# Leftover keys on GpSimd, attention output over two PSUM banks, and a later place for weight loads in a fused pooled-attention and MLP kernel

## The chip, the cores and the metric

One core of one Trainium2 chip. The metric is the device time of one execution in microseconds (us). Spans of the profile are about 1.7 us shorter than device times. TensorE, VectorE, ScalarE and GpSimd stand as PE, DVE, ACT and POOL in the profile; the queues that issue DMAs are SPq (SyncE), ACTq and POOLq.

## The reference, cut to what matters

```python
def _attn_ref(q, k, v):                         # (8, 8, 576, 64): batch, heads, sequence, head dim
    k_p = k.reshape(B, H, 72, 8, D).mean(axis=3)  # keys and values pooled by 8
    v_p = v.reshape(B, H, 72, 8, D).mean(axis=3)
    scores = scale * np.matmul(q, k_p.transpose(0, 1, 3, 2))
    ...                                           # softmax
    return np.matmul(attn, v_p)

def _moe_ref(x, w_in, w_out):                   # x: 4608 tokens of 512, w_in 512x2048
    h = x @ w_in
    g = h - np.tanh(h)
    return g @ w_out
```

So every batch needs its q, k and v loaded, k and v pooled, 72 pooled keys per head scored, and the result, 576 tokens, sent through two dense layers. The kernel handles the tokens in nine groups of 512.

## The kernel before

A group is 16 steps of h (four 128x512 matmuls each, then a tanh and a subtraction) and 16 steps of the output (four matmuls each). The attention of the next batch is woven between these matmuls. That works for groups 1 to 8. At the start there is nothing to weave it into: batch 0's attention must be done before group 0, and the weights arrive while group 0 runs. w1 (the first layer's weights) comes in four chunks of 512 KB, each for four steps of h; w2 likewise. GpSimd issues them; they are cast to bf16 on the way.

The first loads, with their queues:

```python
    load_main(k_pairs, k_raw[0], 0, 0, 1)               # SyncE: batch 0's keys, in three parts
    load_q0(0, 2)                                       # ScalarE: q by heads
    ...
    load_q0(4, 8)
    load_dense(k_pairs, k_raw[0], 0, nc.scalar)         # leftover keys: the last 16 of 144 rows of each head pair
    load_dense(v_pairs, v_raw[1], 0, nc.scalar)         # leftover values
    ...
    nc.gpsimd.memset(q_bf[64:128, R, :, :], 0.0)
    ...                                                 # masks
    nc.gpsimd.dma_start(out=v_bf[:, 0:NM, :], in_=v_pairs[0, 0:128, :, :])   # batch 0's v
    ...
    for c in range(4):
        load_w1(c)
    load_w2(0)
    nc.gpsimd.tensor_copy(out=v_bf[:, NM, :], in_=v_raw[1][:, NM, :])
    load_w2(1)
    ...
    after(load_k(1), w1_dmas[1])        # SyncE: batch 1's k behind w1's second chunk
    load_q(1, False)
    load_main(v_pairs, v_raw[1], 1, 0, NM)
```

Keys are pooled by three adds (4+4, 2+2, 1+1), tile by tile on VectorE; the leftovers are the fifth tile. The output of attention (AV) is then made in eight half blocks, each normalized on VectorE. Between them some steps of h are opened: the first two of their four matmuls run early, and the other two, the second halves of h, follow when AV is done. (kT are the pooled keys transposed, VB the pooled values as AV reads them; the q tail is the last 64 of a head's 576 rows of q.)

```python
    pool_k(0, nc.vector, 2, 4)
    warm_pe(6)                          # matmuls on zeros that fill a wait
    k_turn(2, 4)                        # transposes on TensorE, copies on VectorE
    pool_k(0, nc.vector, NM, NT)        # the leftover keys
    ...
    av_half(0, 0, 0, xs[0], ps_all)     # 3 matmuls, a reciprocal, a multiply
    ...                                 # eight of these, transposes and opened h between them
    for i in range(5, NHID):
        mlp_h(0, i, gts)
        if i == 7:
            q_pe_tail(0)                # the last 64 tokens of batch 0, inside h
        ...
        if i == 13:
            x_pe_transpose(0, 4, x4)
```

The softmax here doesn't subtract the row's maximum and nothing guards it: scores larger than these inputs give would overflow.

## Time and profile before

| | before |
|---|---|
| time, median of the first 3 runs | 300.77 us (300.72 to 301.53) |
| span in the profile | 299.1 us |
| AV's first matmul | 14.61 us |
| second halves of h begin | 21.27 us |
| group 1 begins | 54.98 us |
| w1's last chunk lands | 26.5 us |
| batch 1's v lands | 40.8 us |

The prediction below shows the lines that the starts of AV and of the second halves come from. In each row the first number behind the stretch is its length, then come busy us and, in brackets, instructions of PE, PEld, DVE, ACT and POOL, then the granted clock, the DMA share and GB/s.

```profile
core 0: us, PE busy (x) PEld busy (x) DVE busy (x) ACT busy (x) POOL busy (x), PEclk, DMA share, GB/s
0.00:14.60 14.60, 12.60 (x71) 5.56 (x71) 8.93 (x27) 8.64 (x15) 10.67 (x27) 1.00 0.99 239
14.60:21.30 6.70, 5.72 (x54) 3.59 (x55) 4.59 (x17) 2.85 (x9) 0.00 (x0) 1.00 1.23 212
21.30:55.00 33.70, 32.87 (x233) 17.13 (x232) 22.67 (x51) 21.68 (x39) 13.44 (x8) 1.00 1.11 281
55.00:240.00 185.00, 185.00 (x1046) 90.43 (x1045) 100.52 (x217) 91.92 (x180) 91.34 (x75) 1.00 0.72 177
```

Read it from the bottom. From 55 us on TensorE is busy for 185.00 of 185 us at full clock, so nothing that ends before can do more than move this block. Group 0 (third row) has 0.83 us without a matmul, the two waits of 0.32 and 0.52 us that the prediction names. The first two rows, 21.3 us, are what a change to the start can shorten, and there the DMA engines' mean busy share is 0.99 and more. (Packets are counted at their start, so a share can exceed 1.)

### The profile page before, as it was taken

The page shows a single profiled execution, that of the slowest core. Times are in us where ns is not written, and L with a number is a line of the kernel's source. Part 1 is how long each engine was busy: PE and PEld are TensorE (multiplying, and loading weights), DVE is VectorE, ACT ScalarE, POOL GpSimd, SP SyncE. Part 2 cuts the span into 40 slices and gives each one's busy share as a digit, 9 for nine tenths or more (in the row PEclk, how much of TensorE's full clock was granted, in tenths as well). Part 3 has the DMA queues.
Part 4 walks back from the last instruction along what each step waited for, and adds up shares of the span by engine and source line. Part 5 has one row for each costly group of instructions (what it writes and reads, how often), then busy time and mean ns, then how long its engine had stood idle before and what let it go on. Part 6 is the DMA issues. An engine that isn't in the chain of part 4 may idle for free.

```text
span 299.1 us, 4694 instructions
## 1 busy us (share of the span) xinstructions
PE 291.5 (97%) x1671; PEld 142.5 (48%) x1671; DVE 159.1 (53%) x343; ACT 149.4 (50%) x283; POOL 115.5 (39%) x110
## 2 busy tenths in 40 slices
PE   7989999999999999999999999999999999999994
PEld 3454455544544454445444554455445544444443
DVE  5658665673547444753476247716680758108600
ACT  4647583666146633654265516650665166126511
POOL 8500904871496109922971089307940000000000
PEclk9999999999999999999999999999999999999999
DMA  7999999849854998699648974897431430111032
GB/s 251 226 211 278 311 227 310 263 87 328 234 113 99 271 297 134 117 302 245 107 88 235 300 167 94 242 294 159 97 66 35 95 92 0 37 70 36 0 72 70
DMA packets 66183, 49.79 MB, mean 166 GB/s; under 512 B 39920, under 2 KB 52976, under 8 KB 66160
## 3 DMA queue, kind: packets, MB, share of 16 engines
q1 hardware_dynamic: 58832, 42.94, 56.0%
q0 software_dynamic: 4752, 4.72, 9.4%
q10 hardware_dynamic: 2576, 1.84, 2.3%
q8 instruction: 13, 0.21, 0.3%
q14 instruction: 10, 0.08, 0.1%
HBM read 36.70 MB, written 9.44 MB: 154 GB/s over the span
## 4 chain that ended last, share of the span: by engine, by line
PE 85%; DMA 9%; POOL 4%; issue 0%; SPq 0%; ACT 0%; DVE 0%; POOLq 0%
PE o_ps L456 40%; PE hT_ps L428 37%; DMA w1b<-in_moe_w_in_dram 4%; PE x_ps L346 4%; DMA k_raw<-in_k_dram 4%; PE s_ps L298 3%; POOL k_raw L198 1%; DMA out_dram<-o_sb 1%; POOL k_raw L203 1%; POOL kd L206 1%; POOL w2b L510 0%; PE xT_ps L390 0%; POOL v_raw L576 0%; PE qT_ps L171 0%; POOL w1b L503 0%
## 5 line engine op out<-in xcount | busy, mean ns | idle before, releaser
L456 PE MATMUL o_ps<-w2b,gT 128*128 128x512 bf16 x560 | 134.4, 380 | 0.0
L441 DVE TENSOR_TENSOR gT<-hT_ps,t_sb 128x512 bf16<-128x512 f32 x144 | 98.9, 691 | 57.7 <-ACT t_sb L439 57.6
L428 PE MATMUL hT_ps<-xT,w1b 128*128 128x512 bf16 x576 | 126.9, 379 | 0.3 <-ACT xT L397 0.3
L439 ACT ACTIVATE t_sb<-hT_ps 128x512 f32<-128x512 f32 x144 | 85.6, 597 | 38.3 <-PE hT_ps L428 37.5
L428 PEld LDWEIGHTS <-w1b 128*128 128x128 bf16 x576 | 55.9, 98 | 66.5 <-issue 0.4
L456 PEld LDWEIGHTS <-gT 128*128 128x128 bf16 x560 | 52.5, 98 | 52.0 <-issue 1.4
L465 ACT COPY o_sb<-o_ps 128x512 f32<-128x512 f32 x33 | 19.3, 585 | 75.2 <-PE o_ps L456 75.2
L359 DVE RECIPROCAL rden<-x_ps 128x4 f32<-128x4 f32 x80 | 14.2, 177 | 52.5 <-PE x_ps L346 52.0
L360 DVE TENSOR_TENSOR x_sb<-x_ps,rden 128x256 bf16<-128x256 f32 x80 | 34.0, 425 | 3.5 <-DMA xT<-x_sb 0.6
L148 POOL CAST q_bf<-q_raw 128x2048 bf16<-128x2048 f32 x6 | 11.3, 1888 | 59.9 <-issue 34.8
L198 POOL TENSOR_TENSOR k_raw<-k_raw 128x1280 f32<-128x1280 f32 x7 | 20.2, 2886 | 27.4 <-DMA k_raw<-in_k_dram 16.6
L317 ACT ACTIVATE E<-s_ps 128x288 bf16<-128x288 f32 x60 | 21.4, 410 | 13.2 <-PE s_ps L298 13.0
L346 PE MATMUL x_ps<-VB,E 128*128 128x130 bf16 x240 | 20.8, 221 | 0.4 <-ACT xT L397 0.3
L346 PEld LDWEIGHTS <-E 128*128 128x128 bf16 x240 | 16.9, 98 | 8.8 <-DVE VB L230 0.6
L216 POOL TENSOR_TENSOR v_raw<-v_raw 128x1280 f32<-128x1280 f32 x6 | 17.4, 2898 | 0.0
L298 PE MATMUL s_ps<-qT,KB 128*128 128x288 bf16 (+5 forms) x128 | 17.0, 290 | 0.2
L298 PEld LDWEIGHTS <-KB 128*128 128x128 bf16 (+1 forms) x128 | 7.0, 96 | 10.2 <-issue 3.5
L527 PE MATMUL warm_ps<-xT 128*128 128x512 bf16 x29 | 10.2, 465 | 1.3 <-DVE xT L539 1.3
L206 POOL TENSOR_TENSOR kd<-k_raw 128x640 bf16<-128x640 f32 x7 | 10.8, 1540 | 0.5
L203 POOL TENSOR_TENSOR k_raw<-k_raw 128x640 f32<-128x640 f32 x7 | 10.8, 1541 | 0.5
L397 ACT CAST xT<-xT_ps 128x256 bf16<-128x256 f32 (+1 forms) x14 | 5.8, 436 | 8.5 <-PE xT_ps L390 5.1
L219 POOL TENSOR_TENSOR v_raw<-v_raw 128x640 f32<-128x640 f32 x6 | 9.3, 1544 | 0.5
(73 smaller groups left out, 100.7 us busy)
## 6 DMA issues: line engine op xcount, KB each, us to landing
k_raw<-in_k_dram SPq DMA_DIRECT2D x7, 1024.0 KB, 5.9
q_raw<-in_q_dram SPq DMA_DIRECT2D x7, 1024.0 KB, 10.2
v_raw<-in_v_dram SPq DMA_DIRECT2D x7, 1024.0 KB, 9.3
out_dram<-o_sb SPq DMA_DIRECT2D x38, 128.0 KB, 2.4
out_dram<-o_sb SPq DMA_DIRECT2D x16, 256.0 KB, 3.7
w1b<-in_moe_w_in_dram POOLq DMA_DIRECT2D x4, 512.0 KB, 14.2
w2b<-in_moe_w_out_dram POOLq DMA_DIRECT2D x4, 512.0 KB, 16.9
k_raw<-in_k_dram SPq DMA_DIRECT2D x7, 128.0 KB, 5.8
```

The source lines that it names most:

```text
L198: first = eng.tensor_tensor(out=r[:, :, 0:4, :], in0=r[:, :, 0:4, :], in1=r[:, :, 4:8, :], op=ALU.add)
L216: eng.tensor_tensor(out=r[:, :, 0:4, :], in0=r[:, :, 0:4, :], in1=r[:, :, 4:8, :], op=ALU.add)
L298: nc.tensor.matmul(dst[p : p + w], lhsT=KB[b % 2][:, o : o + w], rhs=qTs[b][:, m, c0:c1], start=True, stop=True,)
L317: nc.scalar.activation(out=E[:, t, half * hs : (half + 1) * hs], in_=ps[:, :], func=ACT.Exp, scale=SCALE)
L346: nc.tensor.matmul(ps[:, 2 * n : 2 * n + 2, :].rearrange("p h d -> p (h d)") if n < 2 else ps.rearrange("p (a s) d -> p a s d", s=2)[:, :, ...
L359: nc.vector.reciprocal(out=rden[:, :, :], in_=ps[:, :, D:D1])
L360: nc.vector.tensor_tensor(out=x_sb[:, half, :, :], in0=ps[:, :, 0:D], in1=rden[:, :, :].to_broadcast([128, 4, D]), op=ALU.mult,)
L428: nc.tensor.matmul(h_tiles[i][:, :], lhsT=w1b[:, fb, i * 128 : (i + 1) * 128], rhs=xT[:, fb, tok0 : tok0 + TG], start=(fb == 0), stop=(fb ...
L439: nc.scalar.activation(out=t_sb[:, :], in_=h_ps[:, :], func=ACT.Tanh)
L441: nc.vector.tensor_sub(out=gT[:, :], in0=h_ps[:, :], in1=t_sb[:, :])
L456: nc.tensor.matmul(o_ps[:, :], lhsT=gts[i][:, tb * 128 : (tb + 1) * 128], rhs=w2b[:, i, :], start=(i == 0), stop=(i == NHID - 1),)
L465: (nc.vector.tensor_copy if g == 0 and tb % 2 else nc.scalar.copy)(out=o_sb[:, :], in_=o_ps[:, :])
```

## The change

Its intent is to shorten the start and to take the waits out of group 0. Five things move at once:

```diff
 # 1. GpSimd: w1 in three chunks, leftover keys pooled, the memset moved behind the load of v
-    nc.gpsimd.memset(q_bf[64:128, R, :, :], 0.0)
     nc.gpsimd.memset(mask[:, :, :], 1.0)
     ...
     nc.gpsimd.dma_start(out=v_bf[:, 0:NM, :], in_=v_pairs[0, 0:128, :, :])
+    nc.gpsimd.memset(q_bf[64:128, R, :, :], 0.0)
     ...
-    for c in range(4):
+    for c in range(3):
         load_w1(c)
-    load_w2(0)
+    pool_k(0, nc.gpsimd, NM, NT)
     nc.gpsimd.tensor_copy(out=v_bf[:, NM, :], in_=v_raw[1][:, NM, :])
-    load_w2(1)
 # 2. w1's last chunk and w2 behind batch 1's k and q; batch 1's v behind w2's first chunk
-    after(load_k(1), w1_dmas[1])
-    load_q(1, False)
-    load_main(v_pairs, v_raw[1], 1, 0, NM)
+    k1 = load_k(1)
+    after(k1[:1], w1_dmas[1])
+    load_dense(v_pairs, v_raw[1], 1)
+    load_q_tail(0)                       # was issued by ScalarE at 8 us
+    load_q_nine(1, 0, nc.sync)
+    load_q_nine(1, 1, nc.sync)
+    load_w1(3)
+    after(w1_dmas[3:], w1_dmas[2])
+    load_w2(0)
+    load_w2(1)
+    after([load_main(v_pairs, v_raw[1], 1, 0, NM)], w2_dmas[0])
+    pool_k(1, nc.gpsimd, 0, NM)
+    load_w2(2)
+    pool_k(1, nc.gpsimd, NM, NT)
+    load_w2(3)
 # 3. AV in four pairs of blocks, each over two PSUM banks
+    def av_pair(p, half, b0):
+        ps = PS[:, b0 : b0 + 2, 0 : 4 * D1].rearrange("p k (h d) -> p k h d", d=D1)
+        for k in range(2):
+            av_mms(0, 2 * p + k, half, ps[:, k, :, :])
+        ...                              # one reciprocal, one multiply for both
 # 4. batch 0's last 64 tokens: AV and transposes in the output's first steps
+        if i == 11:
+            q_cast_tail(0, nc.scalar.copy)
+        if i == 12:
+            q_four_tail(0)
     ...
         if u == 0:
+            x4 = av(0, 4, ps_any, False)
+        if u == 1:
+            x_pe_transpose(0, 4, x4)
 # 5. batch 1's q loaded as nine rows per partition, with no separate tail of 256-byte packets
+    q_nine = q.rearrange("b (s a h) (p j) d -> b s p a h (j d)", s=2, a=2, j=NJ)
 # cut: PSUM as one tile with a helper that hands out its banks; fewer filler matmuls; the five loads
 # that ScalarE issued between 13 and 17 us (batch 1's leftover values, q tail) are gone from its queue
```

## The prediction

> **What bounds the kernel now.** I read the page's busy shares and 40 slices first, then the chain that ended last in order of time, then the timelines of TensorE, VectorE, ScalarE and GpSimd over the first 56 us, then each load's time to landing.
>
> ```profile
> PE 291.5 (97%) x1671; PEld 142.5 (48%) x1671; DVE 159.1 (53%) x343; ACT 149.4 (50%) x283; POOL 115.5 (39%) x110
> ...
> PE   7989999999999999999999999999999999999994
> ...
> DMA  7999999849854998699648974897431430111032
> ```
>
> TensorE is full from the fourth slice on. From 55 us to the end a group is 64 + 64 matmuls of 128x512 plus the next batch's attention, with no wait; a change to the start can only move that block as a whole. The DMA row is also full for the first 50 us, so the loads' order matters. The chain shows where the start still hangs on data:
>
> ```profile
> 5.86 12.86 DMA w1b<-in_moe_w_in_dram
> 18.73 0.38 SPq L102
> 19.21 10.84 DMA k_raw<-in_k_dram
> ...
> 30.21 2.90 POOL k_raw L198
> 33.11 1.47 POOL w2b L510 x2
> 34.58 1.58 POOL k_raw L203
> 36.23 1.55 POOL kd L206
> 37.82 0.45 PE kT_ps L259 x5
> ```
>
> k of batch 1 lands at 30.05, GpSimd pools it until 37.78, and TensorE's transposes wait for that. After them the chain is TensorE alone. In TensorE's timeline the places that matter are:
>
> ```profile
> 11.95 0.60 PE L527 MATMUL warm_ps<-xT 128*128 128x512 bf16 x2
> ...
> 14.61 0.69 PE L346 MATMUL x_ps<-VB,E 128*128 128x130 bf16 x9
> 15.70 0.29 PE L390 MATMUL xT_ps<-ident,x_sb 128*128 128x128 bf16 x2 [0.39 <-DVE x_sb L360]
> ...
> 20.41 4.91 PE L428 MATMUL hT_ps<-xT,w1b 128*128 128x512 bf16 x22
> ...
> 32.75 0.23 PE L390 MATMUL xT_ps<-ident,x_sb 128*128 128x64 bf16 x2 [0.32 <-DVE x_sb L360]
> ...
> 37.82 0.45 PE L259 MATMUL kT_ps<-ident,kd 128*128 128x128 bf16 x5 [0.52 <-POOL kd L206]
> ```
>
> Before 20 us TensorE looks busy, but 29 of its matmuls (L527) are fillers on zeros that stand where it would otherwise wait: the real limits are the other engines' steps. The 22 matmuls from 20.41 are two opened pairs (4), then second halves, so the second halves of h start at 20.41 + 4 x 0.216 = 21.27. Two waits of 0.32 and 0.52 us follow. VectorE in the same stretch:
>
> ```profile
> 10.47 0.43 DVE L198 TENSOR_TENSOR k_raw<-k_raw 128x256 f32<-128x256 f32 x1
> 10.93 0.58 DVE L203 TENSOR_TENSOR k_raw<-k_raw 128x128 f32<-128x128 f32 x1
> 11.54 0.29 DVE L206 TENSOR_TENSOR kd<-k_raw 128x128 bf16<-128x128 f32 x1
> ...
> 15.00 0.18 DVE L359 RECIPROCAL rden<-x_ps 128x4 f32<-128x4 f32 x1
> 15.22 0.42 DVE L360 TENSOR_TENSOR x_sb<-x_ps,rden 128x256 bf16<-128x256 f32 x1
> ```
>
> The leftover keys occupy it from 10.47 to 11.83, although they landed at 9.7; and each of eight half blocks of attention costs a reciprocal and a multiply, 0.55 us from one to the next.
>
> **What the Trainium skill says.** "GPSIMD Engine Reference", Performance versus the Vector engine: a tensor_tensor is about 1.96 times slower on GpSimd. The trace agrees: a 128x1280 add is 2896 ns there, 1493 on VectorE. "SBUF — State Buffer", Who interferes with whom: a VectorE instruction with two SBUF inputs contends with a GpSimd one that reads SBUF. The 0.58 us add above, beside a GpSimd cast, is 0.29 elsewhere. "DMA: Bandwidth & Descriptors", Queues, rings and completion order: each DMA engine takes turns between queues by packets. I counted the trace's packets per us: between 24 and 28 us, the GpSimd queue and SyncE's each moved about 94, which is 95 KB (written as bf16) and 190 KB. The same page, Latency, puts the first byte of a GpSimd-issued DMA at about 1 us; here, under load, w2's third chunk was issued by 33.8 and its first packet started at 37.3, so 3.5 us, which I use.
>
> **The change part by part.**
>
> 1. Leftover keys on GpSimd. They land at 2.37 + 7.3 = 9.7. Scaling GpSimd's 2896, 1552 and 1540 ns to a fifth gives 0.58 + 0.31 + 0.31, about 1.4 with gaps: ready at 11.1 instead of 11.83. The cast of the leftover values waits behind it on GpSimd and ends at 11.9 instead of 11.36, so the pooling matmuls with the spread matrix start at 12.0 instead of 12.39. Two fillers fall away after the leftover transpose and two before AV; the main pooling is cut in two, so that the first VB half is written while the second is pooled. AV starts at about 13.5 instead of 14.61: 1.1 us.
>
> 2. Two-bank AV. Eight reciprocal-and-multiply pairs of 0.55 (4.4 us) become four of 0.18 + 0.69, the latter the time of a 128x512 two-input operation from PSUM here (3.4 us). ScalarE loses the DMA issues that held it: its first xT copy ran at 16.95, after the issue at 16.28, although its transpose was done by 16.0. Then TensorE itself sets the pace: 24 AV matmuls x 0.058, 16 transposes x 0.055, 10 opened h matmuls x 0.216 and 4 fillers x 0.216 are 5.3 us, with some 0.5 of waits. 13.5 + 5.8 = 19.3 against 21.27: 2.0 us gained in all up to here.
>
> 3. Last tokens of batch 0. Their AV and transposes move from h to the output stage; no work is saved. The wait of 0.32 goes, but at the output's second step the transpose needs x_sb: the last tanh and subtraction end 1.5 us after h ends, two half blocks take 0.55 each (2.1 and 2.65), while TensorE arrives at 2.07 (0.86 + 0.35 + 0.86). About 0.45 of wait: +0.13 net.
>
> 4. Batch 1's k earlier, pooled in two pieces: kd is ready near 30 us, needed near 35. The 0.52 wait goes.
>
> 5. Batch 1's q in nines: as many transposing matmul columns as before (16 x 128 + 2 x 128 against 16 x 128 + 4 x 64); its loads no longer have 256-byte packets. One more small matmul for the leftover values, +0.06.
>
> Sum: -2.0 + 0.13 - 0.52 + 0.06 = -2.3 us, or 298.4.
>
> 6. The loads' order takes something back. Alone, a 512 KB weight chunk takes 2.6 us (205 KB/us in the trace at 10 to 12 us); shared with SyncE's queue 5.5 us. Chunk 3 of w1 landed at 26.4 before. Now it waits for chunk 2, which landed at 22.1 and should come near 20, as 256-byte packets of q's tail leave the queue. Issue 0.75, then 3.5: first packet near 24, landing at 27 (beside the small packets of batch 0's q tail, which hardly slow it) to 29.8 (beside batch 1's q). It is needed at h's twelfth step, 19.3 + 2.16 + 7 x 0.864 = 27.5. Then w2's chunk 0 is needed at 31.5, and comes near 32; v of batch 1 may start only after it, lands some 9 us later (41), and VectorE needs 1.49 + 0.82 + 0.22 + 0.42 + 0.69 + 0.42 = 4.1 us for it. VB is ready at 45.1 against a need at 31.5 + 12.5 = 44. These three waits are not added: a wait at the first lets the next load arrive. I put them together at 0.9 us, between 0 and 2.5.
>
> 298.4 + 0.9 = 299.3 us.
>
> **The rivals.** (a) All loads are in time: 298.4 or a little less. For it: every load but w1's last is needed later than it landed before. (b) w1's last chunk is shared with q all the way and TensorE waits over 2 us at the twelfth step: 300.5 to 301, no gain. For it: the DMA row, full in these slices, and 3.5 us before a first packet. Against it: chunk 3 stands behind small packets. (c) The gain meets a later wait: in group 1 batch 2's keys are placed at 68.18 and its scores come at 70.52, 2.3 us of slack; batch 2's k waits for w2's third chunk at about the same time as before (41.8). A gain up to 2.3 passes; more would be cut off, so about 298.4 is a floor. (d) All PSUM is one tile now; if its dependencies were coarser, each group would stall. The built program's waits are of the same kinds in later groups, so I give it little; it would cost several us per group.
>
> **Range and chances.** (a) with a small plus sets the low end at 298.0, (b) the high end at 300.8. Two per cent is 6 us. The whole prologue until 21.3 us has perhaps 3 us to give, so faster by over 2% is nearly impossible; slower needs (d) or a stall of 8 us. Faster 0.01, within 0.975, slower 0.015.
>
> **What would show it right or wrong.** AV's first matmul near 13.5 and second halves of h near 19.3 show steps 1 and 2; TensorE's waits show step 3 (0.45 at the last tokens' transpose, none at kT). TensorE waiting for a DMA of w1 at the twelfth step, of w2 at the first output step, or for VB at batch 1's AV shows step 6, and how much. After 60 us no waits: each group's 30.8 us pitch unchanged. I am wrong if AV doesn't start earlier (leftover keys late on GpSimd), or if the block after 60 us changes its pitch.

## The result, and the profile after

The changed kernel took 302.98 us (median of 4 runs, 302.65 to 303.15), before 300.88 (4 runs) beside it. The ratio is 1.0064 (95% interval 1.0046 to 1.0082). A ratio here is the mean time of one kernel's runs over that of the other's in the same rounds, so it is not quite the ratio of the medians quoted. Executions over 1.5% slower than the fastest of the same kernel are left out of the means. The change costs 2.1 us, where 1.5 us of gain was predicted, and the time lies above the predicted range.

The same table of stages for the changed kernel, cut at the same events:

```profile
0.00:15.15 15.15, 11.85 (x75) 5.58 (x75) 7.63 (x24) 8.71 (x15) 9.78 (x27) 1.00 0.99 242
15.15:21.28 6.13, 5.70 (x55) 3.57 (x55) 4.13 (x10) 2.13 (x4) 1.26 (x2) 1.00 1.16 266
21.28:57.30 36.02, 33.32 (x232) 17.22 (x231) 22.67 (x51) 21.79 (x39) 16.77 (x14) 1.00 1.07 266
57.30:242.30 185.00, 185.00 (x1047) 90.47 (x1045) 100.42 (x217) 91.97 (x180) 89.77 (x75) 1.00 0.70 174
```

Three things are to be seen. The block of groups 1 to 8 is as tight as before and only stands 2.3 us later (57.30 against 54.98). AV starts 0.5 us later and its stage is 0.5 us shorter, so the second halves of h begin at 21.28 us, where they began before (21.27). And group 0 takes 36.02 us instead of 33.70. TensorE is busy in it for 33.32 us instead of 32.87, so 2.70 us of it are waits, where 0.83 were. The whole loss comes from there.

TensorE's timeline of the changed kernel names these waits. Columns: start, us, engine, line, operation, tiles; in square brackets the idle time just before and what ended it.

```profile
15.15 1.21 PE L470 MATMUL PS<-VB,E 128*128 128x130 bf16 x18
...
20.42 9.47 PE L543 MATMUL PS<-xT,w1b 128*128 128x512 bf16 x42
31.17 1.04 PE L543 MATMUL PS<-xT,w1b 128*128 128x512 bf16 x4 [1.28 <-DMA w1b<-in_moe_w_in_dram]
...
37.79 0.23 PE L506 MATMUL PS<-ident,x_sb 128*128 128x64 bf16 x2 [0.32 <-DVE x_sb L456]
...
47.28 0.20 PE L332 MATMUL PS<-vl,spread 128*128 128x64 bf16 x1 [0.81 <-DVE vl L322]
...
48.80 0.39 PE L470 MATMUL PS<-VB,E 128*128 128x130 bf16 x4 [0.17 <-DVE VB L356]
```

The 13th step of h waits 1.28 us for w1's last chunk, and batch 1's leftover values and VB wait 0.81 and 0.17 us for v. The kT wait of 0.52 us is gone. The chain that ended last shows how these hang together (start, us, what):

```profile
6.52 13.21 DMA w1b<-in_moe_w_in_dram
20.81 13.36 DMA w2b<-in_moe_w_out_dram
34.18 10.34 DMA v_raw<-in_v_dram
...
57.34 13.93 PE PS L543 x64
```

Before, this chain went through k, GpSimd's pooling and kT, and then through TensorE alone from 37.8 us. Now it is three loads in a row. w1's third chunk lands; only then does GpSimd issue w1's last chunk and, right behind it, w2's first; and batch 1's v is issued when that one has landed. TensorE's own work leads only from 49 us on.

Why w1's last chunk comes so late is to be seen in GpSimd's timeline (same columns):

```profile
20.02 0.79 POOL L618 DMA_DIRECT2D w1b<-in_moe_w_in_dram  x1 [5.50 <-DMA w1b<-in_moe_w_in_dram]
```

GpSimd waited 5.50 us for the third chunk to land before it could issue the fourth. The DMA view of the changed kernel between 19.4 and 22.6 us lists the queues that moved anything (q0 is GpSimd's, q1 SyncE's):

```profile
## 3 DMA queue, kind: packets, MB, share of 16 engines
q1 hardware_dynamic: 732, 1.17, 103.3%
```

q0 does not appear at all; SyncE's queue has the DMA engines to itself. In the trace's packets GpSimd's queue is empty from 19.37 to 22.68 us: 0.65 until GpSimd starts the issue (the landing is reported at 19.73), 0.79 for the issue, 1.87 until the first packet. Then come, by my count of packets, 55 and 49 KB in the next two full microseconds, during and just after the 256-byte packets of batch 0's q tail, and 88 to 97 KB per us beside batch 1's q. As many bytes as the chunk has are under way by 29.3 us, and it is reported as landed at 31.1; for chunks that ran alone this last step took 0.7 us, and why it takes 1.8 here is open.

This trace has the shortest hole. In the five other traces in which w1's last chunk is chained to the third (after_again, a_v1_free, a_dve_left, a_dve_left2, b_w1_late) GpSimd's queue is empty for 5.7 to 6.4 us, 3.6 to 4.6 of them between the end of the issue and the first packet. The transfer behind it is then shorter, 4.9 to 7.3 us instead of 8.4, and the chunk lands at 31.3 to 33.1.

### The profile page after: what moved, and what is told of

The parts are those of the page before. It is cut to its first block, busy times and chain, and to the rows that moved or that the text cites. A ratio compares the mean times of both kernels' runs of the same rounds, so it can differ in the third digit from the quotient of the medians.

```text
span 301.1 us, 4720 instructions
## 1 busy us (share of the span) xinstructions
PE 291.2 (97%) x1674; PEld 142.7 (47%) x1674; DVE 157.3 (52%) x333; ACT 148.9 (49%) x279; POOL 117.6 (39%) x116
## 4 chain that ended last, share of the span: by engine, by line
PE 81%; DMA 13%; POOL 2%; DVE 1%; issue 0%; ACT 0%; SPq 0%; POOLq 0%; DVEq 0%
PE PS L571 37%; PE PS L543 37%; DMA w2b<-in_moe_w_out_dram 4%; DMA w1b<-in_moe_w_in_dram 4%; PE PS L470 4%; DMA v_raw<-in_v_dram 3%; PE PS L414 3%; DMA out_dram<-o_sb 1%; POOL w1b L618 1%; DVE v_raw L316 0%; PE PS L506 0%; POOL v_raw L685 0%; DVE v_raw L319 0%; DVE VB L337 0%; POOL mask L674 0%
## 5 line engine op out<-in xcount | busy, mean ns | idle before, releaser
L571 PE MATMUL PS<-w2b,gT 128*128 128x512 bf16 x560 | 134.6, 379 | 0.0
L556 DVE TENSOR_TENSOR gT<-PS,t_sb 128x512 bf16<-128x512 f32 x144 | 99.1, 691 | 59.1 <-ACT t_sb L554 58.9
L543 PE MATMUL PS<-xT,w1b 128*128 128x512 bf16 x576 | 126.7, 379 | 1.6 <-DMA w1b<-in_moe_w_in_dram 1.3
L554 ACT ACTIVATE t_sb<-PS 128x512 f32<-128x512 f32 x144 | 85.6, 597 | 39.2 <-PE PS L543 38.9
L580 ACT COPY o_sb<-PS 128x512 f32<-128x512 f32 x33 | 19.4, 586 | 75.3 <-PE PS L571 71.1
L456 DVE TENSOR_TENSOR x_sb<-PS,rden 128x256 bf16<-128x256 f32 x72 | 30.6, 425 | 2.5
L284 POOL TENSOR_TENSOR k_raw<-k_raw 128x1280 f32<-128x1280 f32 (+2 forms) x9 | 21.1, 2347 | 21.1 <-DVE VB L337 15.1
L432 ACT ACTIVATE E<-PS 128x288 bf16<-128x288 f32 x60 | 21.4, 409 | 13.2 <-PE PS L414 13.0
L470 PE MATMUL PS<-VB,E 128*128 128x130 bf16 x240 | 20.4, 220 | 0.3 <-DVE VB L356 0.2
L414 PE MATMUL PS<-qT,KB 128*128 128x288 bf16 (+5 forms) x128 | 16.9, 289 | 0.2 <-DVE KB L369 0.2
```

Of the source, the lines that this page charges most:

```text
L284: first = eng.tensor_tensor(out=r[:, :, 0:4, :], in0=r[:, :, 0:4, :], in1=r[:, :, 4:8, :], op=ALU.add)
L414: nc.tensor.matmul(dst[p : p + w], lhsT=KB[b % 2][:, o : o + w], rhs=qTs[b][:, m, c0:c1], start=True, stop=True,)
L432: nc.scalar.activation(out=E[:, t, c0:c1], in_=ps, func=ACT.Exp, scale=SCALE)
L456: nc.vector.tensor_tensor(out=x_sb[:, half, :, :], in0=ps[:, :, 0:D], in1=rden[:, :, :].to_broadcast([128, 4, D]), op=ALU.mult,)
L470: nc.tensor.matmul(ps[:, 2 * n : 2 * n + 2, :].rearrange("p h d -> p (h d)") if n < 2 else ps.rearrange("p (a s) d -> p a s d", s=2)[:, :, ...
L543: nc.tensor.matmul(h_tiles[i][:, :], lhsT=w1b[:, fb, i * 128 : (i + 1) * 128], rhs=xT[:, fb, tok0 : tok0 + TG], start=(fb == 0), stop=(fb ...
```

## The experiments

Theory L (loads): the loss is the new order of loads alone, above all w1's last chunk, which is held for a landing and then stands behind SyncE's loads. Its rival S (start): the start lost its gain because GpSimd is too slow for the leftover keys, and this is what costs. A third, V: the later issue of batch 1's v is what costs. The table has all runs; waits are those on data in TensorE's timeline between 24 and 50 us, w1 and v in us.

| run | AV starts | second halves of h | wait for w1 | other waits | group 1 starts | median us | ratio to before |
|---|---|---|---|---|---|---|---|
| before | 14.61 | 21.27 | none | 0.32, kT 0.52 | 54.98 | 300.77 | |
| after | 15.15 | 21.28 | 1.28 | 0.32, v 0.98 | 57.30 | 302.98 | 1.0064 |
| after_again | 15.03 | 21.17 | 2.17 | 0.32, v 0.42 | 57.51 | 302.99 | 1.0053 |
| a_w1_early | 14.70 | 20.83 | none | q tail 1.91, 0.31 | 56.21 | 302.38 | 1.0055 |
| a_v1_free | 14.95 | 21.08 | 3.42 | w2 0.20, 0.19 | 58.15 | 303.64 | 1.0077 |
| a_dve_left | 15.31 | 21.44 | 2.06 | 0.32, v 0.80 | 58.07 | 303.73 | 1.0093 |
| a_w1_early_dve_left | 14.90 | 21.03 | none | q tail 2.29, 0.32 | 58.37 | 303.96 | 1.0091 |
| a_dve_left2 | 14.72 | 20.86 | 1.92 | 0.32, v 0.66 | 57.20 | 302.93 | 1.0062 |
| a_w1_qtail | 14.95 | 21.08 | none | 0.33, 0.32 | 54.88 | 300.78 | 0.998 |
| a_w1q_again | 14.81 | 20.94 | none | 0.33, 0.32 | 54.73 | 300.77 | 0.9999 |
| a_w1_qtail_dve | 18.07 | 24.20 | none | 0.33, 0.32 | 58.00 | 303.40 | 1.0064 |
| b_w1_late | 14.46 | 21.43 | 1.48 | w2 1.24 | 56.94 | 302.88 | 1.005 |
| b_pool_left | 14.56 | 21.57 | none | 0.32, kT 0.23 | 54.99 | 300.85 | 0.9999 |
| b_v0_early | 14.86 | 21.59 | none | 0.32, kT 0.21 | 54.77 | 300.62 | 1.0004 |
| a_w1q_avsplit | 14.74 | 21.10 | none | 0.33, 0.32 | 54.89 | 301.41 | 1.0021 |
| a_w1q_v0late | 14.53 | 20.66 | none | 0.33, 0.32 | 54.45 | 300.00 | 0.999 |
| a_w1q_v0late_again | 14.15 | 20.28 | none | 0.33, 0.32 | 54.08 | 299.80 | 0.9961 |
| a_best1 | 15.64 | 21.78 | none | 0.32 | 55.08 | 300.23 | 0.9962 |
| a_best1_again | 14.53 | 20.66 | none | 0.32, 0.69 | 54.93 | 300.31 | 0.998 |
| a_best2 | 15.18 | 21.31 | none | 0.32, 0.27 | 55.01 | 300.52 | 0.9975 |

### First round: the loads of w1 and v, and the leftover keys

a_w1_early: the changed kernel with w1's last chunk in the first burst again.

```diff
-    for c in range(3):
+    for c in range(4):
         load_w1(c)
     ...
-    load_w1(3)
-    after(w1_dmas[3:], w1_dmas[2])
```

> The changed kernel with w1's last chunk issued right behind the third, as before the change. Theory (the order of the loads gave the loss): the chunk lands near 25 us instead of 31.1, TensorE's 1.28 us wait at h's thirteenth step goes; w2's first chunk and so batch 1's v come 2 to 3 us sooner, and the 0.8 us wait for the leftover values goes too or shrinks below 0.3. About 2.4 us less than the changed kernel, 300.5 us. Rival (the loss sits in the prologue or in the new PSUM tile): at most 0.5 us less, 302.5 or more.

It took 302.38 us (301.75 to 304.08), ratio 1.0055 [1.0029, 1.0081]. The wait for w1 is gone and another stands in its place, in the same stretch of h:

```profile
32.21 0.29 PE L213 MATMUL PS<-ident,q_bf 128*128 128x64 bf16 x4 [1.91 <-ACT q_bf L190]
```

This is the transpose of batch 0's q tail. The change moved that load from ScalarE's queue at 8 us to SyncE's queue behind batch 1's k, which itself waits for w1's second chunk. With four chunks of w1 ahead, k comes later, and so does the tail (about 31.5 us). So a second load of the change was late, and the first had hidden it.

a_v1_free: the changed kernel with batch 1's v not held for w2's first chunk.

```diff
-    after([load_main(v_pairs, v_raw[1], 1, 0, NM)], w2_dmas[0])
+    load_main(v_pairs, v_raw[1], 1, 0, NM)
```

> The changed kernel with the load of batch 1's v no longer held until w2's first chunk has landed. Theory (the late v costs about 1.1 us by itself): the wait for the leftover values goes, but w2's first chunk now shares the engines with v and lands 1 to 2 us later, so a wait of about 1 us appears at the first output step; in sum between 302.0 and 303.3. Rival (v is late because the DMA engines are full anyway): v lands at the same time and nothing changes. If the wait goes without a new one: 301.8.

303.64 us (301.81 to 304.93), ratio 1.0077 [1.0049, 1.0105]. The waits for v (0.98) are gone, but w1's grew to 3.42 us. Part of this is chance, since the third chunk, before v could touch it, had also landed 1.4 us later in this trace (21.09). after_again, below, tells how much: there the third chunk landed at 21.09 too, the last chunk's first packet came at 25.82 (here 25.78), and the wait was 2.17 us. So v beside the chunk costs some 1.2 us, its landing being 33.07 instead of 31.89. Theory V gets no support: freeing v does not give the time back while w1 is late.

a_dve_left: the changed kernel with the leftover keys on VectorE.

```diff
-    pool_k(0, nc.gpsimd, NM, NT)
     ...
     pool_k(0, nc.vector, 2, 4)
+    pool_k(0, nc.vector, NM, NT)
```

> The changed kernel with the leftover keys of batch 0 pooled on VectorE again. Theory (GpSimd is the slower place, and the waits for loads behind it hide what the start gains): TensorE's leftover transpose runs about 0.8 us sooner, second halves of h begin near 20.5 instead of 21.28, but the wait for w1's last chunk grows by as much, so the time stays within 0.3 us of the changed kernel, 302.7 to 303.1. Rival (the start sets the end): 0.8 us less, 302.2.

303.73 us, ratio 1.0093 [1.0076, 1.0110]. This was a mistake of mine in the edit: the adds stand ahead of the copies of keys 2 and 3 out of PSUM, so VectorE, whose instructions run in program order in this trace, made these copies wait for the leftover keys' landing (10.26; the copies start at 11.83), and TensorE waited 1.27 us for them. It says nothing for or against S. a_dve_left2 below has the right place.

a_w1_early_dve_left: both edits together, with the same mistake.

> Both: w1's last chunk early and the leftover keys on VectorE. Theory: with the wait for w1 gone, the sooner start counts: 0.5 to 0.8 us less than with w1's chunk early alone, about 299.8 us, a little under the kernel before. Rival (leftover keys on GpSimd cost nothing): the same as w1's chunk early alone.

303.96 us, ratio 1.0091 [1.0062, 1.0119]. It shows the q tail's wait again, of 2.29 us, and something more: after it the clock falls. By stretch, TensorE's granted clock is the number before the last two:

```profile
30.00:32.50 2.50, 0.50 (x3) 0.00 (x1) 0.82 (x2) 0.65 (x2) 2.42 (x3) 1.00 1.14 308
...
34.00:36.00 2.00, 2.00 (x13) 0.95 (x12) 0.69 (x1) 1.01 (x2) 1.19 (x3) 0.50 1.05 402
```

The trace's clock record is at half from 33.94 to 37.36 us, 3.4 us long. a_w1_qtail_dve below has the same after a wait of 3.02 us, from 14.12 to 17.53. The length of the wait alone does not decide this: after the waits of 2.17 us in after_again and 3.42 in a_v1_free the clock stayed at 1.00 in the profiled runs. The same thing lies in the spread of a_w1_early: its runs at a mean clock of 1.0 took 301.75 to 302.72 us, the two at 0.994 took 303.82 and 304.08.

### Second round: the right place for the leftover keys, and the q tail

after_again is the changed kernel once more, as a control.

> The changed kernel itself once more, as the control on the chip of the next three runs: 302.6 to 303.4 us, waits of 1.3 us for w1's last chunk and 0.8 us for the leftover values again. If the order of loads sets the time, both waits may differ by up to 1 us from run to run, as landing times do.

302.99 us (302.61 to 303.41), ratio 1.0053 [1.0040, 1.0066]. The same time, though w1's wait is 2.17 instead of 1.28 us and v's 0.42 instead of 0.98: a longer first wait shortens the later one, as the chain of loads says it should.

a_dve_left2: the leftover keys on VectorE behind the copies.

```diff
-    pool_k(0, nc.gpsimd, NM, NT)
     ...
     k_turn(2, 4)
+    pool_k(0, nc.vector, NM, NT)
```

> The changed kernel with the leftover keys of batch 0 on VectorE, this time behind the copies of the other keys, where they stood before the change (the first try put them ahead of these copies and made them wait). Theory (GpSimd is the slower place, but the wait for w1's last chunk hides it): the leftover transpose runs about 0.7 us sooner, the wait for w1 grows by as much, time within 0.4 us of the changed kernel. Rival (the start sets the end): 0.7 us less.

302.93 us (302.71 to 304.17), ratio 1.0062 [1.0043, 1.0080]. AV begins 0.43 and the second halves of h 0.42 us sooner than in the first trace of the changed kernel, and none of it reaches the end:

```profile
31.38 1.04 PE L543 MATMUL PS<-xT,w1b 128*128 128x512 bf16 x4 [1.92 <-DMA w1b<-in_moe_w_in_dram]
```

The wait for w1 grew from 1.28 to 1.92 us. This run shows the rule: as long as TensorE waits for a load, whatever is won before that load only makes the wait longer. So S falls as the cause of the loss.

a_w1_qtail: w1's last chunk in the first burst and the q tail on ScalarE's queue, as both were before. All the rest of the change stays. I call this the mended kernel.

```diff
     # as a_w1_early, and
-    load_q_tail(0)
     ...
     scores_wide(0, (0, 1))
+    nc.scalar.dma_start(
+        out=q_raws[0][:QT, :, R, :], in_=q[0, :, QA:S, :].rearrange("h p d -> p h d")
+    )
```

> The changed kernel with w1's last chunk in the first burst and batch 0's q tail loaded from ScalarE's queue after the first scores, both as before the change. Theory (the loads' order gave the loss, and with w1 early the q tail behind batch 1's k was the next wait, 1.9 us): neither wait appears, v's wait is under 0.3 us, second halves of h still begin near 21 us; 300.2 to 300.9, like the kernel before. Rival (the DMA engines are simply full, whatever the order): another wait of over 1 us appears and the time stays above 301.8.

300.78 us (300.36 to 300.88), ratio 0.998 [0.9967, 0.9993]. Both waits are gone, and v, still held for w2's first chunk, lands at 39.9 us and is waited for by nobody. The 2.2 us are back. So V falls too: v was late because w2's first chunk, which it waits for, stood behind w1's last (34.16 us in the changed kernel, 31.23 here).

a_w1_qtail_dve: the mended kernel with the leftover keys on VectorE in the right place.

> The same, and the leftover keys on VectorE behind the other keys' copies. Theory: the start gains 0.7 us and now no load hides it: 0.5 to 0.9 us less than the run before it, 299.4 to 300.2, under the kernel before. Rival (a load hides it again): no difference to the run before it.

303.40 us, ratio 1.0064 [1.0049, 1.0079], a miss of its own kind. ScalarE stood still in front of its own DMA issue:

```profile
12.27 1.14 ACT L184 CAST q_bf<-q_raw 128x512 bf16<-128x512 f32 x2 [3.13 <-DMA v_raw<-in_v_dram]
```

The issue of the q tail's load ended up behind the landing of the leftover values (ScalarE issued it at 11.57 instead of 8.1 us), and TensorE waited 3.02 us for the casts behind it. The program does not ask for this wait. In the trace this load has the same semaphore (number 109) as the load of the leftover values, which landed at 11.55, and it was issued 0.02 us later; in a_w1_qtail it had number 100, free since 4.47. So moving the three adds changed which semaphore the built program gave to the load. All six runs also show a mean clock of 0.993 or 0.994. The run is void for S.

### Third round: each suspect alone in the kernel before

b_w1_late: the kernel before with only the loads moved.

```diff
-    for c in range(4):
+    for c in range(3):
         load_w1(c)
-    load_w2(0)
     nc.gpsimd.tensor_copy(out=v_bf[:, NM, :], in_=v_raw[1][:, NM, :])
-    load_w2(1)
     ...
     nc.gpsimd.memset(KB[1][:, :], 0.0)
+    load_w1(3)
+    after(w1_dmas[3:], w1_dmas[2])
+    load_w2(0)
+    load_w2(1)
```

> The kernel before with one part alone: w1's last chunk and w2's first two behind batch 1's k, the last chunk held until the third has landed. Theory: k of batch 1 is pooled about 3 us sooner, so the 0.5 us wait for it goes; w1's last chunk lands near 31 us against a need at 30.4, so a wait of about 1 us comes; 0.3 to 1.2 us more than the kernel before, 301.3 to 302.3. Rival (this part isn't to blame): 0.5 us less than the kernel before.

302.88 us (302.70 to 303.14), ratio 1.0050 [1.0035, 1.0065]: the whole loss of the change, from its loads alone. TensorE's timeline has waits for both weights in it. The kT wait of before is gone, since GpSimd has batch 1's keys pooled at 34.18 instead of 37.77:

```profile
32.23 1.90 PE L428 MATMUL hT_ps<-xT,w1b 128*128 128x512 bf16 x8 [1.48 <-DMA w1b<-in_moe_w_in_dram]
...
37.21 2.75 PE L456 MATMUL o_ps<-w2b,gT 128*128 128x512 bf16 x12 [1.24 <-DMA w2b<-in_moe_w_out_dram]
```

b_pool_left: the kernel before with only the leftover keys on GpSimd, behind w2's first issue.

```diff
     load_w2(0)
+    pool_k(0, nc.gpsimd, NM, NT)
     ...
-    pool_k(0, nc.vector, NM, NT)
```

> The kernel before with one part alone: the leftover keys of batch 0 pooled on GpSimd ahead of the cast of the leftover values. Theory (GpSimd takes 1.6 to 1.8 us for what VectorE does in 1.0): keys ready at 11.4 to 11.6 instead of 11.83, but the cast is a microsecond later and the pooling with the spread matrix with it; AV starts 0.3 to 0.6 us later and the time is 0 to 0.5 us more. Rival (as predicted, 1.4 us on GpSimd): 0.3 us less.

300.85 us (300.54 to 303.57), ratio 0.9999 [0.9968, 1.0029]. AV begins at 14.56 instead of 14.61. GpSimd starts the adds 0.7 us sooner (9.78) and takes longer, so the keys are ready at 11.58 instead of 11.83, but TensorE comes to transpose them at 11.85, where 11.89 was: up to AV nothing is won or lost. The time alone would not show this, since the second halves begin 0.30 us later in this trace and the shorter wait for kT (0.23) takes that up; the fourth round tells where these 0.30 come from. The loss of b_w1_late and its return in a_w1_qtail, with the start as in the changed kernel, settle L against S.

a_best1 was a try at a better version: w1 in one burst, the q tail by SyncE ahead of batch 1's k and behind w1's first chunk, its cast one step earlier, the leftover keys on VectorE in the right place.

```diff
     # as a_w1_early and a_dve_left2, and
+    after([load_q_tail(0)], w1_dmas[0])
     k1 = load_k(1)
     ...
-        if i == 11:
+        if i == 10:
             q_cast_tail(0, nc.scalar.copy)
```

> The changed kernel with four repairs: w1's last chunk in the first burst; batch 0's q tail loaded by SyncE ahead of batch 1's k, once w1's first chunk has landed; the leftover keys on VectorE behind the other keys' copies; the tail's cast one step earlier in h. Theory (loads' order, then the start): no wait for w1, the q tail or v; the 0.5 us wait at the tail's transposes goes; about 0.8 us less than with w1 and the q tail alone (300.8): 299.8 to 300.2. Rival (a load takes the place again): 300.8 or more, with a wait of 0.5 us or more for some load before 50 us.

300.23 us (300.14 to 300.64), ratio 0.9962 [0.9948, 0.9976]. a_best2 moves the memset back ahead of the load of batch 0's v as well.

> The same, and the load of batch 0's v issued from GpSimd behind the clearing of the q tail's rows, as before the change (about 0.6 us later). Theory: v's packets then take less from q's and k's last loads, which land near 9.0 and 9.7 us again instead of 9.7 and 10.6; AV starts 0.4 to 0.8 us sooner; 299.2 to 299.8, half a per cent under the kernel before. Rival (v itself is needed there): no difference or 0.3 us more, as the pooling of v waits for it.

300.52 us (299.97 to 301.62), ratio 0.9975 [0.9959, 0.9992]. Its AV begins 0.46 us sooner than a_best1's, and a wait of 0.27 us, which the profile puts down to a later xT copy on ScalarE, takes most of it.

### Fourth round: where the start's gain went

With the loads mended, a gain at the start can reach the end, so the start could be taken apart. Theory E: batch 0's v is issued 0.67 us earlier in the changed kernel (3.01 instead of 3.68 us, since the memset went behind it), and its packets push back q's heads 4 to 7 and the leftover keys. Theory P: only GpSimd's slower adds delay AV. The first evidence is in the landing times. This is the DMA view of ScalarE's issues around 2.4 us in the kernel before; the last column is from issue to landing in us.

```profile
q_raw<-in_q_dram ACTq DMA_DIRECT2D x1, 512.0 KB, 7.1
k_raw<-in_k_dram ACTq DMA_DIRECT2D x1, 128.0 KB, 7.3
```

And the same two in the changed kernel:

```profile
q_raw<-in_q_dram ACTq DMA_DIRECT2D x1, 512.0 KB, 7.9
k_raw<-in_k_dram ACTq DMA_DIRECT2D x1, 128.0 KB, 8.2
```

Nobody moved these two loads, and both land 0.8 to 0.9 us later. All traces of this case say the same: with v issued at 3.0 us (14 traces) the leftover keys land between 10.1 and 11.0, with v at 3.7 (6 traces) between 9.5 and 10.1.

b_v0_early puts this one line of the change into the kernel before.

```diff
-    nc.gpsimd.memset(q_bf[64:128, R, :, :], 0.0)
     ...
     nc.gpsimd.dma_start(out=v_bf[:, 0:NM, :], in_=v_pairs[0, 0:128, :, :])
+    nc.gpsimd.memset(q_bf[64:128, R, :, :], 0.0)
```

> The kernel before with one line moved: the memset of q_bf's padding stands behind the load of batch 0's v instead of ahead of it, so that GpSimd issues this load at about 3.0 instead of 3.7 us. Theory E (the start's expected gain was lost because v's packets, issued earlier, push back q's heads 4 to 7 and the leftover keys): leftover keys land at 10.4 to 10.8 instead of 9.7, their transpose starts 0.7 to 1.0 us later than 11.85, AV at 15.3 to 15.6 instead of 14.5, second halves of h near 22.1, and the time goes up by 0.3 to 0.9 us (part of it may be taken up by the later waits of 0.32 and 0.52). Theory P (only GpSimd's slower adds delay AV, the landing differs by chance): leftover keys land at 9.5 to 9.9, AV 14.4 to 14.7, time same within 0.2 us.

300.62 us (300.53 to 301.74), ratio 1.0004 [0.9982, 1.0026]. The landings move as E says (leftover keys at 10.5 instead of 9.7 us), AV by less than half of that (14.86 against 14.46 to 14.61 in the traces of the kernel before and its two variants with v late), and the time not at all. So E is right on the landings and too large on what follows. The leftover keys' later landing costs nothing here, because VectorE comes to them at 10.47 in both traces; what moves AV by 0.25 us is q's heads 4 to 7 (landed at 9.65 instead of 8.96, transposed from 10.34 instead of 10.08). And the wait for kT took up 0.3 us at the end (0.21 instead of 0.52).

a_w1q_v0late takes the same line out of the mended kernel, and a_w1q_again is its control.

> The changed kernel with its loads mended (w1's last chunk in the first burst, batch 0's q tail from ScalarE's queue), and the memset moved back ahead of the load of batch 0's v (issued at 3.7 again). Theory E: leftover keys land at 9.7 to 10.0, AV starts at 14.2 to 14.5 instead of 14.95, second halves of h at 20.3 to 20.6, and time 0.3 to 0.6 us under the mended kernel's (300.1 to 300.5). Theory P: AV stays at 14.8 to 15.1, time 300.6 to 300.9.

> Control for these three: the mended kernel again. 300.6 to 300.9 us, AV from 14.7 to 15.1, second halves of h 6.13 us later, ratio to before 0.997 to 0.999.

300.00 us (299.77 to 301.61, ratio 0.9990 [0.9956, 1.0023]) against the control's 300.77 (300.27 to 301.16, ratio 0.9999 [0.9982, 1.0017]). In the traces everything from AV to group 1 stands 0.28 us earlier. The times alone do not tell the two apart.

a_w1q_avsplit is the mended kernel with reciprocal and multiply per block again.

```diff
-        nc.vector.reciprocal(out=rden[:, :, :, :], in_=ps[:, :, :, D:D1])
-        nc.vector.tensor_tensor(... both blocks ...)
+        for k in range(2):
+            nc.vector.reciprocal(out=rden[:, k, :, :], in_=ps[:, k, :, D:D1])
+            nc.vector.tensor_tensor(... block k ...)
```

> The mended kernel with one part of the change undone: reciprocal and multiply are done per block again (eight pairs instead of four over two banks). If two-bank AV is what made AV to second halves 6.1 instead of 6.7 us, this stage is 6.5 to 6.8 here and the time goes up by 0.3 to 0.6 us; if the missing DMA issues on ScalarE made it, the stage stays at 6.1 to 6.2 and the time the same.

From AV to the second halves it takes 21.10 - 14.74 = 6.36 us, the control 6.13 and the kernel before 6.66. So the two-bank AV is worth 0.23 us of the 0.53; the rest came with the other differences of this stage. One of them shows in the traces. In the kernel before, ScalarE stands at its issue of batch 1's q tail until batch 0's q tail has landed, since both loads have the same semaphore (100): issue at 16.28, landing at 16.26, and its first xT copy only at 16.95. In the three variants of the kernel before it is the same (issues at 16.38, 16.43 and 16.58, each 0.02 us behind the landing), and in before, b_w1_late and b_pool_left the second halves begin 4.99 to 5.00 us after this issue (5.21 in b_v0_early, whose AV is later). By these traces a landing that the program does not wait for set the end of this stage, b_pool_left's 0.30 us included; no run takes this issue away by itself. The time, 301.41 us (ratio 1.0021 [0.9987, 1.0056]), has two of four runs at a clock of 0.992 and 0.993 and cannot be read more finely.

### Fifth round: the best version, with more rounds

> The mended kernel with batch 0's v issued at 3.7 again, a second time in more rounds, since the first time's interval was wide (0.9956 to 1.0023). If the earlier issue of v is worth the 0.28 us that the trace showed at AV's start, AV starts between 14.4 and 14.7 here, second halves of h between 20.5 and 20.8, and the ratio to before is 0.996 to 0.9985. If the landings' spread between runs is larger than this effect, AV starts at 14.8 or later and the ratio is 0.999 to 1.001.

The mended kernel with v late, again: 299.80 us (299.65 to 300.16, 6 runs) against 300.94 for the kernel before, ratio 0.9961 [0.9937, 0.9986]. Two of the eleven runs of before had a clock of 0.992 (302.78 and 302.89); without them its mean is 300.83, still 1.0 us above. This version beats both kernels. In its trace the leftover keys land at 9.5 us, AV begins at 14.15 and the second halves of h at 20.28, which is 1.0 us sooner than before, and group 1 begins 0.9 us sooner. Its only waits for data in group 0 are 0.33 us for the cast of the q tail, which stands one step too late for its transpose, and the 0.32 us at the last tokens' transpose.

> The version that beat both kernels (w1 in one burst, q's tail from SyncE's queue ahead of batch 1's k, leftover keys on VectorE), again on another day's chip: 300.0 to 300.6 us, ratio to before 0.995 to 0.998 if its gain is its own; 0.999 to 1.001 if it came with that call's slower runs of before. No wait for a load on TensorE.

a_best1 again took 300.31 us (299.97 to 301.08), ratio 0.998 [0.9956, 1.0004]: the time held, the first runs of before had been somewhat slow, and with this interval the gain is not clear of noise. Its AV began 1.1 us sooner than in its first trace (14.53 against 15.64) and a wait of 0.69 us for ScalarE took most of that.

## Why the prediction was wrong

The prediction got the direction of most parts right and their balance wrong. Its own sign of being wrong, that AV doesn't start earlier, came true. Point by point, by its steps.

**Step 1, AV at 13.5 us: it was 15.15.** Three terms are off. The leftover keys were put down at 9.7 us, where the kernel before had them; they landed at 10.5, since the moved memset lets v's packets in earlier (b_v0_early has that line alone, and 10.45). I had seen that line in the diff and not asked what it does to the loads beside it. The three adds on GpSimd were scaled to a fifth, 1.4 us; GpSimd's timeline shows 1.79 from the first start to the last end:

```profile
10.68 0.73 POOL L284 TENSOR_TENSOR k_raw<-k_raw 128x256 f32<-128x256 f32 x1 [3.40 <-DVE KB L366]
11.49 0.45 POOL L289 TENSOR_TENSOR k_raw<-k_raw 128x128 f32<-128x128 f32 x1
12.02 0.45 POOL L292 TENSOR_TENSOR kd<-k_raw 128x128 bf16<-128x128 f32 x1
```

They take 0.73, 0.45 and 0.45 us instead of 0.58, 0.31 and 0.31: a fixed part does not shrink with the tile. From the two adds of one form, 2896 ns for 1280 elements and 730 ns for 256, the slope is 2166 / 1024 = 2.1 ns per element and what is left is about 0.19 us per instruction, an estimate. VectorE's rows in the prediction already show such a part: half the elements took 0.29 us and not half of 0.43. Last, from the leftover keys' transpose to AV it was 15.15 - 12.53 = 2.62 us, with 2.4 assumed. Together 0.8 + 0.4 + 0.2 are 1.4 of the 1.65 us.

**Step 2, second halves at 19.3: they began at 21.28.** Of the 2.0 us gain nothing came. The stage from AV on was to shrink from 6.66 to 5.8 us and shrank to 6.13: the direction was right, its size 0.3 too large, and by a_w1q_avsplit the two banks are worth 0.23 of the 0.53. Even in the best version they begin at 20.28, a gain of 1.0 and not 2.0.

**Steps 3 to 5 held.** The wait at the last tokens' transpose was 0.32 (0.45 predicted, so 0.13 less), kT's wait of 0.52 is gone (kd was ready at 32.5 us, not 30, and still in time), and the additional small matmul takes 0.04 (47.28 to 47.32).

**Step 6, "0.9 us, between 0 and 2.5", is the step that failed and that decides.** It measured 1.28 us for w1 and 0.98 for v, 2.26 in all, near its upper end; w2 was no wait. The failing term is w1's landing, "at 27 ... to 29.8", which was 31.1. It was not the hole: the first packet came at 22.7, sooner than the 24 put down. It was the transfer, 8.4 us where 3.0 (beside the q tail) to 5.8 (beside batch 1's q) were allowed. Both came, one after the other, and the small packets, "which hardly slow it", came with the lower rate (about 50 KB per us, against 88 to 97 beside q). The guess had a ground: in the kernel before, GpSimd's queue moved 155 to 161 KB per us beside such packets on ScalarE's queue. Why it was slower here is open. In the other traces the hole was longer and the transfer shorter, with landings no earlier. The 3.5 us to a first packet were also read from a chunk that stood behind another: by my count it is 3.3 (33.83 to 37.13), and until 35.3 the queue was moving the chunk ahead of it. And the sum was made the wrong way: a start that gains 2.0 us and a load that lands late are not two terms to be added. With the landing at 31.1 the predicted start would have met a wait of 31.1 - 27.5 = 3.6 us (an estimate from the prediction's own need and the measured landing), and the gain would have been gone all the same, as a_dve_left2 shows with its 0.42 us. The end was set by the load's landing plus what follows it.

**Rival (b) was the right one**, "w1's last chunk is shared with q all the way and TensorE waits over 2 us", and even it stands at 300.5 to 301 because it kept the start's gain. In the two traces of the changed kernel the wait is 1.28 and 2.17 us. The prediction set it aside with "chunk 3 stands behind small packets", as if these were cheap. **Rivals (c) and (d)** did not show: groups 1 to 8 have no wait and the same length, and the 0.9 us that the best version gains at group 1 reach the last group.

In balance, from the second halves of h on: +1.28 for w1, +0.98 for v, -0.52 for kT are +1.74. Group 1 begins 57.30 - 54.98 = 2.32 us later. Of the remaining 0.58, 0.45 are longer busy time of TensorE in group 0 (33.32 against 32.87 us, the extra small matmul in it), and 0.13 are gaps too short to be shown as waits; I have not told them apart further. What stays open also is how much of the landings' differences at the start is chance: the same kernel's AV began at 14.53 and 14.15 us in two traces, and at 15.64 and 14.53 in two of a_best1.

## What to carry to other kernels

A load that is waited for fixes the time of everything behind it; what is won ahead of it makes only the wait longer, so size gains and late loads with a maximum and not with a sum. Before a load is chained to another's landing, count the hole that it opens in its queue (here 3.3 to 6.4 us: the report of the landing, the issue, the time to the first packet), then what every queue will be moving by then, in order, and compare the landing with the need. And when a line of setup moves past a DMA issue, ask which other loads now share their first microseconds with it. Last, when an engine that also computes issues a DMA just as an earlier one lands, look whether the two share a semaphore.

## What the Trainium skill lacked or had wrong

- "DMA: Bandwidth & Descriptors", Latency and other measured facts, gives about 1 us to the first byte of a GpSimd-issued DMA. For w1's last chunk the issue took 0.79 us and its first packet came 1.87 us after its end, beside a busy SyncE queue, and in five other traces 3.6 to 4.6 us after it. No page says what chaining a load to a landing costs beside busy queues, 3.3 to 6.4 us of an empty queue here.
- The same page, Why small descriptors are slow, puts the overhead of a 256-byte descriptor at 27%. Beside 256-byte packets on SyncE's queue GpSimd's queue moved 55 KB in the us from 23, and 88 to 97 per us once batch 1's q came; beside those on ScalarE's queue, in the kernel before, it moved 155 to 161. A reader needs to know when such packets slow another queue and by how much.
- "GPSIMD Engine Reference", Performance versus the Vector engine, gives a ratio of 1.96 at one size. Small tiles have another: a 128x256 add took 0.73 us against 0.43 on VectorE (1.7), a 128x128 add 0.45 against 0.29 (1.6), and about 0.19 us per instruction are fixed (estimated from the two sizes above). For small pieces the fixed part is what a plan has to count.
- "TensorE: Matmul & The Clock Gate" lets the clock fall after an idle window of about 3.4 us. Here waits of 2.29 and 3.02 us were followed by a granted clock of 0.50 for 3.4 us, and waits of 2.17 and 3.42 us in other traces were not: a shorter wait than the page's window is not always safe, and what decides stays open.
- No page tells that an engine can stall at its own DMA issue because an earlier DMA still in flight has the same semaphore: 3.13 us of ScalarE in a_w1_qtail_dve, and in the kernel before an issue that comes 0.02 us after the earlier landing (16.28 and 16.26), with no such wait in the program's text.
